# Transposing gathered rows by DMA, as two 16-bit halves, in a kernel of attention followed by routed experts

## The chip, the cores and the metric

The kernel runs on one core of a Trainium2 chip. The core has a matrix engine (TensorE, PE in the profile), three engines for elementwise work (VectorE or DVE, ScalarE or ACT, GpSimd or POOL), a queue engine (SyncE or SP) and 16 DMA engines that all queues share. Each engine runs its own instructions in order; engines wait for each other by semaphores. The metric is the device time of one execution in microseconds (us). Before the change it is 213.47 us, the median of 3 runs from 212.46 to 213.69.

## The reference

There are two stages. The first is an attention with polynomial sketches; its output is put into rows of 128 numbers, one row for each of 4352 tokens. The second sends each row through one of eight experts, which a hash of the token's id selects:

```python
expert_idx = token_ids * np.int64(2654435761) % np.int64(E)
for e in range(E):
    mask = expert_idx == e
    xe = x[mask]
    h = np.maximum(xe @ w1[e], 0.0)
    out[mask] = h @ w2[e]
```

Here `x` is 4352 x 128, `w1[e]` is 128 x 1024 and `w2[e]` is 1024 x 128, all 32-bit floats.

## The kernel before

The attention stage handles four batches one after the other. For each it makes sketch features, sums them into a small matrix (`kv`), multiplies queries by it (`x_ps`), divides by a denominator (`den`, lines 460 and 461), and stores the rows (`xs`, line 466, and the rest of a batch, `xs_tail`, line 480) to a table `x_rows` in memory. Beside it, VectorE and TensorE work out a list of tokens sorted by expert: `get` holds, for each of 36 tiles of 128 slots, the rows to fetch, and `put` the rows to write.

The expert stage works on 16 groups of 288 columns, two for each expert. The first eight groups (18 tiles, 0 to 17) hold only tokens whose rows are stored early, so they can start before the last batch is done; tiles 18 to 35 need the whole table.

- **Gather.** `gather` (line 549) is an indirect DMA that GpSimd issues: 128 rows of 128 numbers into a tile `xg`. The tiles come from a pool of six buffers (line 576).
- **Transpose.** `bring` (lines 582 to 592) takes three gathered tiles at a time. TensorE transposes each of them into a bank of PSUM, `xp` (line 589). `evict` (line 553) copies the bank to columns of `xT`: ScalarE takes the even calls and VectorE the odd ones. `xT` is kept in blocks of nine tiles (1152 columns, four groups), in two buffers (line 569); so there are four blocks, and block 2 can be written only when block 0 has been read.
- **First product.** For each of eight steps c of a group, `hp` (line 664) is a 128 x 128 piece of `w1` times the group's 288 columns. It goes to one of four PSUM banks. Its relu goes to `hT` by ScalarE for even c (line 555) and by VectorE for odd c (line 557); that frees the bank.
- **Second product.** Interleaved with it, `op` (line 672) sums the eight pieces of the previous group times `w2`.
- **Send.** `send` (lines 644 to 656) lets TensorE turn finished columns back into rows (`tp`, line 650), copies them to `os`, and GpSimd scatters each tile to the output (`out_dram`, line 637).

At step c = 3 of each group g, lines 682 and 683 bring in all tiles up to the end of group g + 1. Up to line 628 the instructions of all engines stand in the order of the program text; that covers the attention stage and the first six gathers. After that line a scheduler decides in which order each engine has its instructions, and the order is then fixed. The pool `moe` (line 632), from which `hT`, `os` and the change's new tiles come, takes the memory that the attention stage's loads have released.

Of the kernel before, what the change touches and what calls it, by code (L numbers as in the profile page):

```python
# [9 lines left out]
F32 = mybir.dt.float32  # L10
BF16 = mybir.dt.bfloat16
I32 = mybir.dt.int32
AF = mybir.ActivationFunctionType
OP = mybir.AluOpType
AX = mybir.AxisListType
# [2 lines left out]
def _words(ap):  # L18

    t = dataclasses.replace(ap.tensor, shape=list(ap.tensor.shape))  # L20
    return t.bitcast(I32)


@with_exitstack
def kernel(
# [12 lines left out]
    nc = tc.nc  # L38
    P = 128
    B, H, S, D = q.shape  # L40
    R = S1.shape[0]
    N, DM = out.shape
# [13 lines left out]
    GN = 288  # L56
    EB = B - 2
    EP = (EB * S + SM // 2) // C
    NE = EP * C
    HT = E * GN // P  # L60
    ST = 2 * HT
# [6 lines left out]
    rows_in = ctx.enter_context(tc.tile_pool(name="rows_in", bufs=6))  # L68
# [14 lines left out]

    s64 = const.tile([2 * R, D, 2], I32)
    for i, s in enumerate((S1, S2)):
        nc.sync.dma_start(s64[i * R:(i + 1) * R], _words(s).rearrange("r (d two) -> r d two", two=2))
    tok = const.tile([P, C, 2], I32)
    nc.scalar.dma_start(tok[:], _words(moe_token_ids).rearrange("(p c two) -> p c two", p=P, two=2))

    def load_tail(src, name, eng):  # L90
# [82 lines left out]

    def s_tile(name, dt=I32):
        return const.tile([2 * R, D], dt, name=name)
# [53 lines left out]
    in_tile = hots.tile([P, C, ST], BF16)  # L229
    put = const.tile([P, ST], I32)  # L230
    get = const.tile([P, ST], I32)

# [315 lines left out]
    def gather(dst, idx, rows=N):  # L548
        nc.gpsimd.indirect_dma_start(  # L549
            out=dst[:], out_offset=None, in_=x_dram[0:rows],  # L550
            in_offset=bass.IndirectOffsetOnAxis(ap=idx, axis=0), bounds_check=rows - 1, oob_is_err=False)

    def evict(n, dst, src, relu=False):
        if n % 2 == 0:
            nc.scalar.activation(dst, src, AF.Relu if relu else AF.Copy)  # L555
        elif relu:
            return nc.vector.tensor_scalar(dst, src, 0.0, None, op0=OP.max).ins  # L557
        else:
            nc.vector.tensor_copy(dst, src)


    BG, BT = 4, 4 * GN // P
    assert BG * GN == BT * P and ST % BT == 0
    xTs, oTs = {}, {}

    def columns(of, pool, name, lo, hi):
        b = lo // (BT * P)
        if b not in of:
            of[b] = pool.tile([P, BT * P], F32, tag=name, name=name, bufs=2)
        return of[b][:, lo - b * BT * P:hi - b * BT * P]  # L570
# [3 lines left out]
    def fetch(upto):  # L574
        for i in range(len(xgs), upto):
            xg = rows_in.tile([P, DM], F32, tag="xg", name="xg")
            gather(xg, get[:, i:i + 1], NE if i < HT else N)
            xgs.append(xg)

    done_in = done_out = 0  # L580

    def bring(upto):
        nonlocal done_in
        while done_in < upto:
            n = min(3, ST - done_in)
            fetch(done_in + n)
            xp = ps_x.tile([P, 4, P], F32, tag="x", name="xp")
            for i in range(n):
                nc.tensor.transpose(xp[:, i], xgs[done_in + i][:], ident[:])  # L589
            evict(done_in // 3, columns(xTs, rows_in, "xT", done_in * P, (done_in + n) * P),  # L590
                  xp[:, 0:n].rearrange("p a b -> p (a b)"))
            done_in += n


    b, e = EB, EB + 1
# [24 lines left out]
    for g in range(GQ):  # L620
        x_products(e, g, fTs[g], last_m)
    bring(3)
    x_tail_products(e, last_m)
    denominators(e, 0, GQ * HQ + H)
# [7 lines left out]
    moe = ctx.enter_context(tc.tile_pool(name="moe", bufs=3))  # L632
# [11 lines left out]
    def send(upto):  # L644
        nonlocal done_out
        while done_out + 1 <= upto:
            n = min(2, upto - done_out)
            tp = ps_x.tile([P, 4, P], F32, tag="x", name="tp")
            for i in range(n):
                nc.tensor.transpose(tp[:, i], columns(oTs, moe, "oT", (done_out + i) * P, (done_out + i + 1) * P), ident[:])  # L650
            os = moe.tile([P, 2, DM], F32, tag="os", name="os", bufs=3)
            evict(done_out // 2, os[:, 0:n], tp[:, 0:n])
            for i in range(n):
                sent = scatter(os[:, i], put[:, done_out + i:done_out + i + 1])
            done_out += n
        return sent
# [3 lines left out]
    def layer1(g, c):  # L660
        if c == 0:
            hTs[g] = moe.tile([P, FC, GN], F32, tag="hT", name="hT", bufs=2)
        hp = bank([P, GN], "hp")
        nc.tensor.matmul(hp[:], w1[:, g % E, c * P:(c + 1) * P], columns(xTs, rows_in, "xT", g * GN, (g + 1) * GN), start=True, stop=True)  # L664
        return evict(c, hTs[g][:, c], hp[:], relu=True)
# [3 lines left out]
    def layer2(g, c, lo=0, hi=GN):  # L669
        if c == 0:  # L670
            ops[g] = ps_o.tile([P, GN], F32, tag="o", name="op")
        nc.tensor.matmul(ops[g][:, 0:hi - lo], w2[:, g % E, c], hTs[g][:, c, lo:hi], start=(c == 0), stop=(c == FC - 1))  # L672
        if c == FC - 1:
            nc.scalar.copy(columns(oTs, moe, "oT", g * GN + lo, g * GN + hi), ops[g][:, 0:hi - lo])  # L674

    G = 2 * E
    for g in range(G):
        for c in range(FC):
            last = layer1(g, c)
            if g > 0:  # L680
                layer2(g - 1, c)
            if c == 3:
                bring(min(ST, -(-((g + 2) * GN) // P)))
            if c == 3 and g > 1:
                sent = send((g - 1) * GN // P)
                if g % 4 == 3:

                    with tc.issue_after(sent):
                        nc.gpsimd.drain()
        if g == G - 4:  # L690
            tables_after = last
# [38 lines left out]
    with tc.For_i(0, turns) as j:  # L730
# [25 lines left out]
        xg = rows_in.tile([P, DM], F32, tag="xg", name="xg")  # L756
# [6 lines left out]
        for i in range(FH):  # L763
            hp = bank([P, 512], "hp")
            nc.tensor.matmul(hp[:], xr[:], w1f[:, bass.ds(e + i * 512, 512)], start=True, stop=True)
            nc.scalar.activation(hs[:, i * 512:(i + 1) * 512], hp[:], AF.Relu)
        hr = moe.tile([P, FC, P], F32, tag="hT", name="hr", bufs=2)
# [41 lines left out]
```

## Time and profile before

| What | Value |
|---|---|
| Span of the profiled run | 213.5 us |
| TensorE busy | 200.3 us, 94% |
| VectorE, ScalarE busy | 101.3 us (47%), 69.1 us (32%) |
| GpSimd busy | 96.8 us, 45% |
| First gather issued | 62.50 us |
| First hp | 71.27 us |
| Last gather, last scatter issued | 172.15 us, 208.02 us |
| TensorE's end, about | 206.6 us |

A row of the groups view names the line, engine and operation, the tile written and the tile read, the count, then the busy time in us and the mean duration in ns, and last the engine's idle time just before these instructions and what ended it. In the timeline a row begins with its start and the time it covers, both in us. A 32-bit matrix product stands as two records, and records of TensorE overlap, so the distance between starts says more of its pace than the durations. The idle time of an engine which is not the bottleneck costs nothing.

### The profile page before, as it was taken

How to read it: one execution, taken by the hardware profiler on the slowest of the kernel's cores; microseconds unless marked ns; L12 is line 12 of the kernel's file. 1: busy time of each engine (PE TensorE's matmuls, PEld its weight loads, DVE VectorE, ACT ScalarE, POOL GpSimd, SP SyncE). 2: the span in 40 equal slices, each digit the busy share in tenths (PEclk: the TensorE clock that was granted, in tenths of full speed). 3: DMA queues.
4: the chain of work that ended last, by engine and by line, in shares of the span. 5: the costliest groups of instructions: out<-in, count | busy, mean ns of one | idle time of the engine just before them, and what ended most of it. 6: DMA issues, size and time to landing. Idle time of an engine off the chain costs nothing.

```text
span 213.5 us, 3351 instructions
## 1 busy us (share of the span) xinstructions
PE 200.3 (94%) x1178; PEld 164.6 (77%) x1179; DVE 101.3 (47%) x204; ACT 69.1 (32%) x195; POOL 96.8 (45%) x118
## 2 busy tenths in 40 slices
PE   7889999999898989999999999999999999999960
PEld 2779999899788667777777777777777787777850
DVE  4599999999998141223223123132232228232200
ACT  2231843636334223322331242333213233322210
POOL 8253105227028787035467733376741550530371
PEclk9999999999999999999999999999999999999997
DMA  3999899999111331000111100111210100100000
GB/s 112 298 291 328 286 347 339 297 351 344 62 51 49 108 129 49 12 25 25 40 35 39 55 31 15 37 38 40 61 39 0 46 24 14 36 12 12 23 27 24
DMA packets 22177, 22.16 MB, mean 104 GB/s; under 512 B 4186, under 2 KB 19291, under 8 KB 22160
## 3 DMA queue, kind: packets, MB, share of 16 engines
q1 hardware_dynamic: 18496, 17.05, 26.0%
q0 software_dynamic: 2432, 4.72, 7.2%
q10 hardware_dynamic: 1232, 0.17, 0.5%
q8 instruction: 10, 0.16, 0.3%
q14 instruction: 7, 0.06, 0.1%
HBM read 17.47 MB, written 4.59 MB: 103 GB/s over the span
## 4 chain that ended last, share of the span: by engine, by line
PE 48%; DVE 21%; issue 11%; DMA 11%; POOL 4%; ACT 1%; POOLq 1%; SPq 1%; DVEq 0%; ACTq 0%
PE hp L664 22%; PE op L672 19%; DMA out_dram<-os,put 8%; DVE f L354 4%; DVE fT L427 3%; DMA q<-in_q_dram 3%; POOL out_dram L637 3%; DVE kp L354 3%; DVE qT L404 2%; PE kv L379 2%; DVE row L288 2%; PE xp L589 1%; PE x_ps L436 1%; PE tp L650 1%; PE x_ps L447 1%
## 5 line engine op out<-in xcount | busy, mean ns | idle before, releaser
L664 PE MATMUL hp<-xT,w 128*128 128x288 f32 x256 | 82.5, 408 | 1.0 <-DVE hT L557 1.0
L672 PE MATMUL op<-hT,w 128*128 128x288 f32 (+2 forms) x272 | 82.1, 392 | 0.0
L557 DVE TENSOR_SCALAR hT<-hp 128x288 f32<-128x288 f32 x64 | 29.3, 457 | 84.0 <-PE hp L664 65.6
L672 PEld LDWEIGHTS op<-hT,w 128*128 128x128 f32 x272 | 49.8, 191 | 12.4
L549 POOL DMA_INDIRECT xg<-x_rows,get x36 | 37.5, 1040 | 44.2 <-PE xp L589 16.1
L664 PEld LDWEIGHTS hp<-xT,w 128*128 128x128 f32 x256 | 47.1, 190 | 13.4 <-DVE hT L557 1.5
L637 POOL DMA_INDIRECT out_dram<-os,put x36 | 35.9, 996 | 36.9 <-ACT os L555 18.9
L555 ACT ACTIVATE hT<-hp 128x288 f32<-128x288 f32 x64 | 26.1, 410 | 61.0 <-PE hp L664 47.6
L466 POOL TENSOR_TENSOR xs<-xe,den 128x512 f32<-128x512 f32 x6 | 7.7, 1297 | 20.3 <-DVE den L461 12.6
L436 PE MATMUL x_ps<-m,fT 128*128 128x132 f32 x128 | 15.8, 280 | 0.0
L379 PEld LDWEIGHTS kv<-va,kp 128*128 128x128 f32 x128 | 14.7, 192 | 0.9 <-issue 0.7
L379 PE MATMUL kv<-va,kp 128*128 128x66 f32 x128 | 14.8, 274 | 0.5 <-DVE kp L354 0.5
L436 PEld LDWEIGHTS x_ps<-m,fT 128*128 128x128 f32 x128 | 14.8, 190 | 0.3
L398 ACT COPY m<-kv 32x66 f32<-32x66 f32 x48 | 9.9, 205 | 11.4 <-PE kv L379 10.8
L674 ACT COPY oT<-op 128x288 f32<-128x288 f32 (+2 forms) x17 | 6.5, 384 | 19.0 <-PE op L672 12.8
L354 DVE TENSOR_TENSOR f<-ab 128x1024 f32<-128x1024 f32 (+1 forms) x9 | 11.6, 1289 | 0.1
L427 DVE STREAM_TRANSPOSE fT<-f 128x1024 f32<-128x1024 f32 (+1 forms) x9 | 11.2, 1244 | 0.7
L354 DVE TENSOR_TENSOR kp<-ab 128x1024 f32<-128x1024 f32 x8 | 9.3, 1242 | 0.0
L342 PE MATMUL ab_ps<-s_k,kT 128*128 128x64 f32 (+1 forms) x72 | 9.1, 275 | 0.0
L165 PE MATMUL idle<-warm 128*128 128x512 bf16 x21 | 7.8, 486 | 1.4 <-POOL warm L137 1.4
L342 PEld LDWEIGHTS ab_ps<-s_k,kT 128*128 128x128 f32 (+1 forms) x72 | 8.6, 191 | 0.5 <-issue 0.2
L413 PE MATMUL abq_ps<-s_k,qT 128*128 128x64 f32 (+1 forms) x72 | 8.5, 269 | 0.4 <-DVE qT L404 0.4
(138 smaller groups left out, 151.2 us busy)
## 6 DMA issues: line engine op xcount, KB each, us to landing
w<-in_moe_w_dram SPq DMA_DIRECT2D x16, 512.0 KB, 8.1
k<-in_k_dram SPq DMA_DIRECT2D x4, 512.0 KB, 4.6
v<-in_v_dram SPq DMA_DIRECT2D x4, 512.0 KB, 7.9
q<-in_q_dram SPq DMA_DIRECT2D x3, 512.0 KB, 7.7
x_rows<-xs SPq DMA_DIRECT2D x3, 512.0 KB
xg<-x_rows,get POOLq DMA_INDIRECT x36
out_dram<-os,put POOLq DMA_INDIRECT x36
q<-in_q_dram SPq DMA_DIRECT2D x2, 256.0 KB, 6.9
```

Of the source, the lines that this page charges most:

```text
L342: nc.tensor.matmul(ab_ps[:, g:g + w, h].rearrange("p t x r -> p t (x r)"), kT[:w * D, h], s_k[:w * D, 0:w].rearrange("p t x r -> p (t x r) ...
L354: eng.tensor_tensor(dst, ab[:, :, 0].unsqueeze(3).to_broadcast(shape), ab[:, :, 1].unsqueeze(2).to_broadcast(shape), op=OP.mult)
L379: nc.tensor.matmul(kv[:, pr], kp[rows, t, 2 * pr:2 * pr + 2].rearrange("p h i j -> p (h i j)"), va[rows, t, 2 * pr:2 * pr + 2].rearrange(" ...
L398: copy(m[f][t * D:(t + 1) * D, h::2, t], src)
L427: nc.vector.transpose(fT[r].rearrange("p k (q s) -> p k q s", q=Q), f[r].rearrange("p q h (k d) -> p (h k) q d", d=D))
L436: nc.tensor.matmul(p[:, h], fT[:, (h0 + h) * FB + fb], m[fb][:, h0 + h].rearrange("p t d -> p (t d)"), start=(fb == 0), stop=(fb == FB - 1 ...
L549: nc.gpsimd.indirect_dma_start(out=dst[:], out_offset=None, in_=x_dram[0:rows], in_offset=bass.IndirectOffsetOnAxis(ap=idx, axis=0), bound ...
L555: nc.scalar.activation(dst, src, AF.Relu if relu else AF.Copy)
L557: return nc.vector.tensor_scalar(dst, src, 0.0, None, op0=OP.max).ins
L637: st_ = nc.gpsimd.indirect_dma_start(out=out[:], out_offset=bass.IndirectOffsetOnAxis(ap=idx, axis=0), in_=src[:], in_offset=None, bounds_ ...
L664: nc.tensor.matmul(hp[:], w1[:, g % E, c * P:(c + 1) * P], columns(xTs, rows_in, "xT", g * GN, (g + 1) * GN), start=True, stop=True)
L672: nc.tensor.matmul(ops[g][:, 0:hi - lo], w2[:, g % E, c], hTs[g][:, c, lo:hi], start=(c == 0), stop=(c == FC - 1))
```

## The change

The tiles of the first block (0 to 8) are brought in as before. All later tiles go another way: three gathers fill one tile `xg3`; two copies split each 32-bit word into its two 16-bit halves, `xh`; one DMA transpose on SyncE's queue turns all six 128 x 128 pieces of 16-bit words into `xh_turned`; two more copies join the halves in `xT`. It is meant to take the transposes of 27 tiles from TensorE. So that the longer way has time, tiles are brought in one group earlier: at c = 3 of group g, up to the end of group g + 2. `xg3` has three buffers, `xh` and `xh_turned` two each.

```diff
+def _half(ap, x):
+    return ap.bitcast(U16).rearrange("p (n two) -> p n two", two=2)[:, :, x]
...
             n = min(3, ST - done_in)
+            if done_in >= BT:
+                xg = moe.tile([P, 3, DM], F32, tag="xg3", name="xg3", bufs=3)
+                for i in range(n):
+                    gather(xg[:, i], get[:, done_in + i:done_in + i + 1], NE if done_in + i < HT else N)
+                xh = moe.tile([P, 2, 3 * DM], U16, tag="xh", name="xh", bufs=2)
+                tt = moe.tile([P, 2, 3, P], U16, tag="xh_turned", name="xh_turned", bufs=2)
+                for x in range(2):
+                    evict(done_in // 3, xh[:, x, 0:n * DM], _half(xg[:].rearrange("p a b -> p (a b)"), x)[:, 0:n * DM])
+                assert n == 3
+                nc.sync.dma_start_transpose(tt[:].rearrange("p x a b -> p (x a) b"), xh[:].rearrange("p x b -> p (x b)"))
+                to = columns(xTs, rows_in, "xT", done_in * P, (done_in + n) * P)
+                for x in range(2):
+                    evict(done_in // 3, _half(to, x), tt[:, x].rearrange("p a b -> p (a b)"))
+                done_in += n
+                continue
             fetch(done_in + n)
...
             if c == 3:
-                bring(min(ST, -(-((g + 2) * GN) // P)))
+                bring(min(ST, -(-((g + 3) * GN) // P)))
```

In the changed program's own line numbers the gather is line 555, the relus are lines 561 and 563, the split and join copies 561 and 565, the DMA transpose 602, the TensorE transpose 611, hp 686 and op 694.

More of the change, by code (lines that the diff above doesn't have):

```diff
@@ L12 @@
 I32 = mybir.dt.int32
+U16 = mybir.dt.uint16
 AF = mybir.ActivationFunctionType
```

## The prediction

> **What bounds the kernel now.** I read the page first: its chain that ended last, and its groups of instructions. One core gives the time, 213.5 us in the profile and 213.47 us as the median.
>
> ```profile
> PE hp L664 22%; PE op L672 19%; DMA out_dram<-os,put 8%; DVE f L354 4%; DVE fT L427 3%; DMA q<-in_q_dram 3%; POOL out_dram L637 3%; DVE kp L354 3%; DVE qT L404 2%; PE kv L379 2%; DVE row L288 2%; PE xp L589 1%; PE x_ps L436 1%; PE tp L650 1%; PE x_ps L447 1%
> ...
> L664 PE MATMUL hp<-xT,w 128*128 128x288 f32 x256 | 82.5, 408 | 1.0 <-DVE hT L557 1.0
> L672 PE MATMUL op<-hT,w 128*128 128x288 f32 (+2 forms) x272 | 82.1, 392 | 0.0
> ...
> L549 POOL DMA_INDIRECT xg<-x_rows,get x36 | 37.5, 1040 | 44.2 <-PE xp L589 16.1
> ```
>
> The two expert matrix products (hp, op) head the chain, and the idle time before them is 1.0 us and 0.0 us. GpSimd issues 36 gathers, with 44.2 us idle before them. Next the stages, by the view of windows:
>
> ```profile
> core 0: us, PE busy (x) PEld busy (x) DVE busy (x) ACT busy (x) POOL busy (x), PEclk, DMA share, GB/s
> 71.00:78.00 7.00, 5.89 (x28) 3.96 (x27) 2.64 (x7) 1.80 (x5) 5.63 (x8) 1.00 0.17 49
> 95.00:112.00 17.00, 17.00 (x77) 13.49 (x76) 4.66 (x11) 4.78 (x12) 8.42 (x9) 1.00 0.10 28
> 112.00:200.00 88.00, 88.00 (x388) 68.76 (x387) 27.25 (x67) 24.93 (x63) 41.66 (x42) 1.00 0.10 32
> ```
>
> From 78 us on TensorE has no gap at full clock; VectorE and ScalarE are under a third busy, the DMA engines a tenth. So in the expert stage each TensorE instruction removed is time gained, and each wait that holds up TensorE is time lost. Only the entry (71 to 78 us) has gaps. The timeline gives the price of a transpose:
>
> ```profile
> 96.94 0.65 PE L672 MATMUL op<-hT,w 128*128 128x288 f32 x2
> 97.43 0.49 PE L589 MATMUL xp<-ident,xg 128*128 128x128 f32 x3
> 97.76 0.38 PE L650 MATMUL tp<-ident,oT 128*128 128x128 f32 x2
> 97.97 0.65 PE L664 MATMUL hp<-xT,w 128*128 128x288 f32 x2
> ```
>
> Durations overlap, so I use starts. Three gathered tiles take 97.76 - 97.43 = 0.33 us, 0.11 us each. One hp or op (two records) takes 0.485 us, so one step c of a group (an hp and an op) takes 0.97 us. The same view at the entry:
>
> ```profile
> 70.03 1.00 POOL L549 DMA_INDIRECT xg<-x_rows,get  x1 [0.30 <-issue]
> ...
> 71.33 1.00 POOL L549 DMA_INDIRECT xg<-x_rows,get  x1 [0.30 <-issue]
> 72.64 1.00 POOL L549 DMA_INDIRECT xg<-x_rows,get  x1 [0.30 <-issue]
> ...
> 73.31 0.78 PE L589 MATMUL xp<-ident,xg 128*128 128x128 f32 x3
> ...
> 73.94 1.00 POOL L549 DMA_INDIRECT xg<-x_rows,get  x1 [0.30 <-issue]
> ```
>
> Gathers leave every 1.30 us, and TensorE is already at their heels: tile 5 (issued 70.03) is transposed about 73.76. I call gathered tiles 0 to 35; groups of 288 columns g; block 0 is tiles 0 to 8, groups 0 to 3.
>
> **What the Trainium skill says.** "VectorE: DVE Perf Modes", The three transpose paths, gives 1309 ns for a 128x128 bf16 transpose by DMA and 390 ns by TensorE; in this trace TensorE's cost 0.11 us in a row, so only the ordering agrees, and no DMA transpose is in the trace. "DMA: Bandwidth & Descriptors", Latency and other measured facts, gives 261 GB/s for such transfers. The same page, DMA Transpose (X-bar), limits them to 2-byte elements, which is why each 32-bit word is split. The same page, Rules for kernel authors, has a DMA that reads what another wrote wait for its completion; here gathers of tiles 18 up wait for the last batch's rows to be stored, and the trace shows a 256 KB store landing in 2.0 us.
>
> **The change, part by part.**
> 1. Removed from TensorE: 27 transposes x 0.11 = 2.9 us, all on the gapless part: -2.9 us. Their evictions (nine of 128x384: ScalarE 0.49, VectorE 0.56) go too.
> 2. Added: four copies of 128x384 for each of nine triples (two split, two join). No row shows a strided 16-bit copy; I take 0.49 as ScalarE's row, bounds 0.42 and 0.6. That is 36 x 0.49 = 17.6 us over two engines with over 60% idle in this stage. Their duration alone is hidden.
> 3. Added: nine transfers of 196 KB on SyncE's queue. Lower bound 2 us (196 KB / 261 GB/s = 0.75 us of data; the 256 KB store's 2.0 us), upper bound 6 x 1.309 = 7.9 us, both estimates from the page and the store row. I take 4 us, nearer the store.
> 4. Moved, and this decides. ScalarE and VectorE run in order and also free the four PSUM banks of hp: a copy waiting for a gather holds the relu behind it, and TensorE stops about four steps later. GpSimd's queue is in order too. In the built program's order GpSimd issues tiles 0-5, then **tiles 9-15, then 6-8**, then the last batch's rows, then 16-35; every scatter follows. TensorE has tile 6's transpose ahead of hp(g=0, c=4), tile 7's ahead of c=5, tile 8's ahead of c=6, because block 0 is now brought in one group earlier.
>
> Entry: the gathers from 71.33 on are tiles 9, 10, ..., 15, 6, 7, 8. Tile 8 leaves at 71.33 + 9 x 1.30 = 83.06 instead of 73.94. For landing I take 3.3 us from the issue's start, range 2.9 to 3.7 (tile 5 above gives 3.7; the rows' tail, which waits for tile 8, starts 77.09, so at most 3.15 there). Tile 8 lands at 86.4; hp(0,6) 86.5, hp(1,1) 88.4. Before, hp(1,1) starts 78.45, and 0.33 more with tiles 6-8 transposed already, as they now are: +9.7 us. VectorE's copies for tiles 9-11 (landed 77.2) and ScalarE's for 12-14 (81.2) hold their relus too, but end earlier, so they hide in this wait.
>
> Groups 1 and 2: the last batch's rows (2.1 + 0.4 us on GpSimd) wait for tile 8 and end 86.8; stored and landed by about 89.5 (2.0 to 4 us). Tile 18 can leave then. Twelve gathers at 1.30 put tile 29 at 89.5 + 11 x 1.30 = 103.8, landed 107.1. VectorE has the copies for tiles 27-29 right after relu (2,1) and ahead of relu (2,3): copies to 108.1, relu to 108.6. hp(2,7) needs that bank, so it starts 108.6. Before it starts at 92.58, with the same nine tiles transposed: +16.0 us in all. Waits between (tile 17, 91.5; the third transfer, about 96; tile 23, about 99; tile 26, about 103) lie inside that sum. Later copies have their gathers landed (tile 35 at about 115) and wait for a transfer alone, with some 3 us of slack: nothing at 4 us.
>
> Scatters: the first leaves at about 113 instead of 90.5. By then four to six tiles are due, at 1.30 us each against 2.25 tiles per 8 us: caught up long before the end. TensorE's end to the span's end, 213.5 - 206.6 = 6.9 us, stays.
>
> Sum: 213.5 + 16.0 - 2.9 = **226.5 us**.
>
> **Rivals.**
> - All hidden, as intended: tiles 6-8 are needed only for columns 576 up, so the earlier order costs nothing: 213.5 - 2.9 = 210.6. For: DMA a tenth busy, helpers idle. Against: gathers leave 1.30 us apart and seven stand ahead of tile 6, on the one engine that issues them. Faster; 4%.
> - Only the entry's wait: copies of groups 1 and 2 fit in the slack of four banks: 213.5 + 9.7 - 2.9 = 220.3. For: VectorE is mostly idle. Against: tile 29's landing. 15%.
> - Slow transfers, 7.9 us: the transfer of tiles 21-23, from about 104, must release the buffer that 27-29 split into (+4), and in groups 4 and 8 the joining copy stands two or one relus behind the one that starts its transfer (+2.5 each): about 236. For: the only price per tile. Against: the store row. 14%; slower still, with transfers queueing behind each other, 5%.
> - The forecast: 60%. Another 2% for gains and losses that cancel.
>
> **How the numbers follow.** The forecast moves with landing (0.8 us over its range), store (2 us) and copies (1 us): 223 to 230. The low end reaches the entry-only case less its landing error, 219.5; the high end the 7.9 us transfers and a little, 238. Outside lie the hidden case, the very slow one, and parts of others. Faster by over 1% 4%, within 1% 2%, slower 94%.
>
> **What would show it.** Right: TensorE idle some 10 us between hp(0,3) and hp(0,7), ended by gathers; tile 8's gather near 83; then idle before hp in groups 1 and 2 laid to VectorE and ScalarE relus behind copies; hp(2,7) near 108; gapless after, at 0.97 us a step without L589 rows; transfers landing in 2 to 6 us. Wrong: gathers closer than 1.3 us, an entry gap under 7 us, or idle that recurs in groups 4 and 8 (slow transfers). Largest risk: a transfer's duration, which no row before shows.

## The result, and the profile after

The changed kernel takes 229.75 us (median of 4 runs, 227.43 to 230.6), the kernel before 213.12 us beside it (212.46 to 213.69). The ratio is 1.076, with a 95% interval of 1.068 to 1.085: slower, by some 16 us. The profiled run has a span of 228.9 us. Times of later kernels are compared with the kernel before as run on the same chip (213.8 to 214.4 us). Some runs come out slower at a lower clock; they are left out of every ratio, though not of the medians.

The page first, its slices and its groups:

```profile
PE   7979999999989049968799999999999999999980
...
PEclk9999999999999755999799999999999999999995
...
L686 PE MATMUL hp<-xT,w 128*128 128x288 f32 x256 | 86.2, 423 | 4.9 <-DVE hT L563 4.2
L694 PE MATMUL op<-hT,w 128*128 128x288 f32 (+2 forms) x272 | 83.6, 398 | 0.0
...
L555 POOL DMA_INDIRECT xg<-x_rows,get x36 | 37.1, 1030 | 22.9 <-DVE f L360 10.4
...
L611 PE MATMUL xp<-ident,xg 128*128 128x128 f32 x9 | 2.4, 337 | 9.8 <-DMA xg<-x_rows,get 9.7
```

TensorE has a hole in the 14th and 15th slices (74 to 86 us), and thinner slices from there to about 114 us; the clock falls to 0.5 in the 15th and 16th. The idle time is 9.8 us before the nine transposes that are left, and 4.9 us before hp, where it was 1.0. Next the stages, cut as before at 71, 95, 112 and 200 us, with the piece between 78 and 95 added:

```profile
core 0: us, PE busy (x) PEld busy (x) DVE busy (x) ACT busy (x) POOL busy (x), PEclk, DMA share, GB/s
71.00:78.00 7.00, 3.00 (x21) 2.25 (x19) 1.00 (x4) 0.68 (x2) 5.22 (x6) 0.96 0.19 49
78.00:95.00 17.00, 11.24 (x32) 7.56 (x33) 3.88 (x11) 4.77 (x11) 11.91 (x13) 0.62 0.40 103
95.00:112.00 17.00, 12.10 (x48) 8.62 (x47) 4.56 (x13) 4.45 (x12) 13.04 (x14) 0.99 0.34 73
112.00:200.00 88.00, 88.00 (x372) 68.70 (x371) 27.51 (x71) 27.62 (x69) 27.91 (x29) 0.98 0.11 31
```

All of TensorE's idle time in these stretches lies before 112 us. From 95 to 112 us TensorE works 12.1 of 17 us instead of all of them. Between 78 and 95 us the granted clock is 0.62, a second loss that busy time does not show. After 112 us TensorE is full again. In none of these stretches are the DMA engines half busy. Who holds it up is in the timelines. GpSimd first:

```profile
71.54 1.00 POOL L555 DMA_INDIRECT xg<-x_rows,get  x1 [0.30 <-issue]
...
83.42 0.99 POOL L555 DMA_INDIRECT xg<-x_rows,get  x1 [0.30 <-issue]
84.42 2.06 POOL L472 TENSOR_TENSOR xs<-xe,den 128x512 f32<-128x512 f32 x2
87.03 0.40 POOL L486 TENSOR_TENSOR xs_tail<-xe,den 64x128 f32<-64x128 f32 x1 [0.54 <-POOL xs L472]
...
92.13 1.00 POOL L555 DMA_INDIRECT xg<-x_rows,get  x1 [2.05 <-DMA x_rows<-xs_tail]
...
106.44 1.00 POOL L555 DMA_INDIRECT xg<-x_rows,get  x1 [0.30 <-issue]
...
115.53 1.02 POOL L659 DMA_INDIRECT out_dram<-os,put  x1 [0.30 <-issue]
```

These are, by count, tile 9's gather (71.54), tile 8's (83.42), the last batch's rows, tile 18's gather, which waits until the rows are stored, tile 29's (106.44), and the first scatter. TensorE beside it:

```profile
73.51 0.49 PE L611 MATMUL xp<-ident,xg 128*128 128x128 f32 x3
83.38 0.45 PE L611 MATMUL xp<-ident,xg 128*128 128x128 f32 x1 [9.38 <-DMA xg<-x_rows,get]
...
86.60 0.47 PE L611 MATMUL xp<-ident,xg 128*128 128x128 f32 x1 [0.37 <-DMA xg<-x_rows,get]
...
103.07 0.75 PE L686 MATMUL hp<-xT,w 128*128 128x288 f32 x2 [2.33 <-DVE hT L563]
...
107.18 0.75 PE L686 MATMUL hp<-xT,w 128*128 128x288 f32 x2 [0.71 <-ACT hT L561]
...
110.28 0.75 PE L686 MATMUL hp<-xT,w 128*128 128x288 f32 x2 [1.87 <-DVE hT L563]
...
112.14 1.17 PE L694 MATMUL op<-hT,w 128*128 128x288 f32 x2
```

First it waits 9.38 us for tile 6's rows, then three times for a relu: hp(2,3) at 103.07, hp(2,6) at 107.18, hp(2,7) at 110.28. A relu takes under half a microsecond, so the question is what the relu's engine was doing. VectorE:

```profile
102.00 0.66 DVE L565 COPY xh<-xg 128x384 uint16<-128x384 uint16 x2 [5.09 <-DMA xg<-x_rows,get]
102.58 0.81 DVE L563 TENSOR_SCALAR hT<-hp 128x288 f32<-128x288 f32 x2
...
109.23 0.63 DVE L565 COPY xh<-xg 128x384 uint16<-128x384 uint16 x2 [5.85 <-DMA xg<-x_rows,get]
109.78 0.81 DVE L563 TENSOR_SCALAR hT<-hp 128x288 f32<-128x288 f32 x2
```

It was idle, for 5.09 and 5.85 us: a split copy stood first in its queue and waited for a gather, with two relus behind it. TensorE's hp starts 0.49 and 0.50 us after those relus start. Between these two, hp(2,6) waited for ScalarE, which shows the same:

```profile
105.90 0.94 ACT L561 ACTIVATE xh<-xg 128x384 uint16<-128x384 uint16 x2 [6.54 <-DMA xg<-x_rows,get]
106.74 0.39 ACT L561 ACTIVATE hT<-hp 128x288 f32<-128x288 f32 x1
```

So it is not true here that the idle time of an engine which is not the bottleneck costs nothing: work that TensorE needed stood behind it.

The new transfers and the copies that join the halves:

```profile
L565 DVE COPY xT<-xh_turned x10: 375/380/390, 81.6 to 157.0; 128x384 uint16<-128x384 uint16 x10
L602 SPq DMA_TRANSPOSE xh_turned<-xh x9: 1210/1219/1328, 77.8 to 153.9; - x9
L561 ACT ACTIVATE xT<-xh_turned x8: 605/620/643, 88.4 to 153.3; 128x384 uint16<-128x384 uint16 x8
...
DMA to landing us min/median/max: 2.7/3.0/3.8
```

A transfer of 196 KB lands 3.0 us after its issue (2.7 to 3.8), and SyncE takes 1.2 us to issue it.

The description of the kernel before needs one correction. Ahead of line 628 the text order holds for the instructions written there, but the scheduler also puts later gathers and copies among them. In the changed kernel that is where the gathers of tiles 9 to 15 and the first split copies stand.

### The profile page after: what moved, and what is told of

Same layout as the page of the kernel before. It is cut to its first block, busy times and chain, and to the rows that moved or that the text cites. A ratio compares the mean times of both kernels' runs of the same rounds, so it can differ in the third digit from the quotient of the medians.

```text
span 228.9 us, 3338 instructions
## 1 busy us (share of the span) xinstructions
PE 202.5 (88%) x1151; PEld 164.6 (72%) x1152; DVE 103.4 (45%) x219; ACT 74.3 (32%) x207; POOL 96.1 (42%) x118
## 4 chain that ended last, share of the span: by engine, by line
issue 34%; POOL 15%; DMA 11%; POOLq 2%
POOL out_dram L659 9%; DMA out_dram<-os,put 7%; POOL xg L555 6%; DMA xg<-x_rows,get 2%; DMA x_rows<-xs_tail 2%; POOLq L711 2%; POOL xs L472 1%; POOLq L659 0%; POOL xs_tail L486 0%; POOLq L555 0%; POOLq L486 0%; POOLq L752 0%
## 5 line engine op out<-in xcount | busy, mean ns | idle before, releaser
L686 PE MATMUL hp<-xT,w 128*128 128x288 f32 x256 | 86.2, 423 | 4.9 <-DVE hT L563 4.2
L694 PE MATMUL op<-hT,w 128*128 128x288 f32 (+2 forms) x272 | 83.6, 398 | 0.0
L659 POOL DMA_INDIRECT out_dram<-os,put x36 | 35.4, 983 | 74.5 <-ACT os L561 44.2
L686 PEld LDWEIGHTS hp<-xT,w 128*128 128x128 f32 x256 | 49.2, 199 | 18.4 <-DVE hT L563 5.1
L694 PEld LDWEIGHTS op<-hT,w 128*128 128x128 f32 x272 | 50.7, 193 | 13.2
L565 DVE COPY xh<-xg 128x384 uint16<-128x384 uint16 x10 | 3.2, 363 | 22.3 <-DMA xg<-x_rows,get 13.3
L611 PE MATMUL xp<-ident,xg 128*128 128x128 f32 x9 | 2.4, 337 | 9.8 <-DMA xg<-x_rows,get 9.7
L611 PEld LDWEIGHTS xp<-ident,xg 128*128 128x128 f32 x9 | 1.3, 155 | 11.8 <-ACT hT L561 9.6
L561 ACT ACTIVATE xh<-xg 128x384 uint16<-128x384 uint16 x8 | 3.7, 511 | 17.9 <-DMA xg<-x_rows,get 17.9
```

The lines of the kernel that those rows point to most:

```text
L659: st_ = nc.gpsimd.indirect_dma_start(out=out[:], out_offset=bass.IndirectOffsetOnAxis(ap=idx, axis=0), in_=src[:], in_offset=None, bounds_ ...
```

## The experiments

The theory: two orders lose the time. On GpSimd's queue, early gathers of later tiles delay tiles 6 to 8, and with them the rows of the last batch. On VectorE's and ScalarE's queues, split and joining copies wait ahead of relus that TensorE needs. The rivals: the earlier bringing-in costs by itself; or the transfers do, by their duration or by their traffic.

**The earlier lead alone** (lead_alone in the expectations). The kernel before, with its own TensorE transposes and only this:

```diff
-                bring(min(ST, -(-((g + 2) * GN) // P)))
+                bring(min(ST, -(-((g + 3) * GN) // P)))
```

> The kernel before, with only the earlier bringing: at c = 3 of group g the tiles up to the end of group g + 2, all transposed by TensorE. The theory (gathers of later tiles stand ahead of tiles 6 to 8 because their own buffers free them, and copies waiting for gathers hold up relus) expects almost nothing: the gathers still wait for TensorE to free six buffers, so tiles 6 to 8 leave at about 71 to 74 us; tile 8 lands near 76.7, half a microsecond after hp(0,6) could start: about 213.6 us, 213 to 215. A rival, that bringing tiles early is itself the loss because TensorE then waits for them, expects 220 us or more.

Measured: 216.88 us against 214.37 us, ratio 1.015 (1.009 to 1.021). Of its profile, the longest wait of TensorE for a gather, of three that sum to 2.6 us:

```profile
76.72 0.33 PE L589 MATMUL xp<-ident,xg 128*128 128x128 f32 x1 [1.50 <-DMA xg<-x_rows,get]
```

In this kernel the six buffers of `xg` keep later gathers behind tiles 6 to 8, which leave at 70.50 to 73.11 us. From the first hp to the first op it takes 8.39 us (70.44 to 78.83) instead of 6.69 (71.27 to 77.96); 0.33 of that is three transposes that only come earlier, so the lead costs about 1.4 us there. It is more than the theory had. The profiled run took 215.38 us at a mean clock of 0.993; the other three took 216.83 to 217.66 us at 0.979 to 0.981. So the rest of the 1.5% goes with a lower clock, and no trace shows where that drop lies or whether the lead causes it. Even with it, the lead is about a fifth of the whole loss: a part, not the cause.

**The old lead in the changed kernel**, halves and transfers kept:

```diff
-                bring(min(ST, -(-((g + 3) * GN) // P)))
+                bring(min(ST, -(-((g + 2) * GN) // P)))
```

> The changed kernel with its tiles brought in up to the end of group g + 1 again, as before the change; the halves and the transfers stay. If the loss comes from the order on GpSimd's queue and from copies that wait for gathers ahead of relus, the earlier bring is not what costs: in the built program GpSimd still has tiles 9 to 15 ahead of 6 to 8, and every copy of groups 1 and 2 still stands behind the same gathers. Only TensorE's transposes of tiles 6 to 8 come a group later, so it can do four more products before it waits, and then waits as long for the rows: 228 to 230 us. If the earlier bring itself is the loss, which lead_alone makes unlikely, the time falls to 220 or less.

Measured: 227.35 us (226.24 to 228.07) against 213.79, ratio 1.062 (1.055 to 1.070). TensorE's waits in its trace:

```profile
78.95 1.33 PE L686 MATMUL hp<-xT,w 128*128 128x288 f32 x2 [4.04 <-DVE hT L563]
83.31 3.25 PE L686 MATMUL hp<-xT,w 128*128 128x288 f32 x6 [3.03 <-ACT hT L561]
...
101.60 0.87 PE L686 MATMUL hp<-xT,w 128*128 128x288 f32 x2 [2.59 <-DVE hT L563]
102.26 1.17 PE L694 MATMUL op<-hT,w 128*128 128x288 f32 x2
...
108.78 0.75 PE L686 MATMUL hp<-xT,w 128*128 128x288 f32 x2 [1.13 <-DVE hT L563]
```

The wait for tiles 6 to 8 is gone from the entry, and 7 us of waiting for relus behind split copies stand in its place. This is what a chain with two holders looks like: take one away and the other shows. hp(2,7) comes at 108.78, only 1.5 us sooner, because tile 18's gather could leave at 90.50 instead of 92.13. The expectation had TensorE wait for the rows as long as before; it waited for relus instead, which were held by split copies of tiles 9 to 14. The time is a little under the expected 228 us, and the ratio is 1.062 instead of 1.076, so that the lead is again about a fifth of the loss; the rival's 220 us falls.

**Gathers of block 0 first.** In the changed kernel each later gather is queued behind tile 8's; the copies stay where the scheduler puts them:

```diff
+            got.append(gather(xg, get[:, i:i + 1], NE if i < HT else N).ins)
...
+                  with tc.issue_after(got[BT - 1]):
                     gather(xg[:, i], get[:, done_in + i:done_in + i + 1], NE if done_in + i < HT else N)
```

> The changed kernel with one edit: gathers of tiles 9 and up are queued on GpSimd behind that of tile 8. The theory expects the entry's wait of about 10 us gone (tile 8 leaves near 74 us), but VectorE and ScalarE still have the split copies in among the relus as in the changed kernel, so the waits of groups 1 and 2 remain, gated by gathers 1.30 us apart that start at about 77.9: by hand hp(3,1) near 107.6 us against 94.5 before and 113.1 in the changed kernel. With 2.9 us fewer transposes and perhaps 1.5 us of lower TensorE clock: about 224 us, 221 to 226. A rival, that the order of the first gathers is the whole loss, expects 210 to 212; a rival, that transfers and copies cost by themselves, expects no change from about 229.

Measured: 225.36 us (224.25 to 225.47), ratio 1.052 (1.045 to 1.058). Line 688 is hp here, and line 613 the transpose:

```profile
76.54 0.33 PE L613 MATMUL xp<-ident,xg 128*128 128x128 f32 x1 [1.29 <-DMA xg<-x_rows,get]
...
83.96 0.75 PE L688 MATMUL hp<-xT,w 128*128 128x288 f32 x2 [0.78 <-DVE hT L563]
...
88.60 1.33 PE L688 MATMUL hp<-xT,w 128*128 128x288 f32 x2 [3.40 <-ACT hT L561]
...
104.20 0.86 PE L688 MATMUL hp<-xT,w 128*128 128x288 f32 x2 [3.32 <-ACT hT L561]
```

The entry is mended (waits of 0.24, 0.87 and 1.29 us instead of 9.38), and most of the loss stays, as waits for relus. hp(3,1) came at 108.91 us, expected near 107.6. The copies' order is thus a loss of its own.

**Copies late, gathers left.** The reverse: the three stages of a triple are written apart: the three gathers first (`take`), the two split copies and the transfer a group and a step later (`split`), the two joining copies almost a group after that (`join`). The copies are held in the order of the text. Tiles 6 to 8 are brought with the old lead, and GpSimd still has the gathers of tiles 9 to 15 ahead of theirs:

```diff
+    AT = (0, 1, 2, 4, 5, 6, 8, 9, 10)
...
+                if (g, c) == (at, 5):
+                    take(j)
+                if (g, c) == (at + 1, 6):
+                    split(j)
+                if (g, c) == (at + 2, 5):
+                    join(j)
```

> The changed kernel with the work in stages: split copies one group after their gathers and join copies another group later, each queued behind the relus that the program has ahead of it; gathers of tiles 9 to 15 stay ahead of tiles 6 to 8, and TensorE has tiles 6 to 8 at step 3 of group 1, as in the kernel before. The theory expects only the entry's wait: tile 8 lands near 86.6 us where TensorE could use it at 81.4, so 5.2 us, and about 1.9 us for the lower TensorE clock after a gap of over 5 us: 213.1 + 5.2 + 1.9 - 2.9 = 217.3 us, 215.5 to 219, no waits for VectorE or ScalarE later. A rival, that transfers and copies cost by themselves, expects 223 or more.

Measured: 218.77 us, ratio 1.018 (1.010 to 1.027). All of TensorE's waits between 70 and 118 us:

```profile
83.69 0.30 PE L595 MATMUL xp<-ident,xg 128*128 128x128 f32 x1 [3.49 <-DMA xg<-x_rows,get]
84.93 0.47 PE L595 MATMUL xp<-ident,xg 128*128 128x128 f32 x1 [0.93 <-DMA xg<-x_rows,get]
86.38 0.48 PE L595 MATMUL xp<-ident,xg 128*128 128x128 f32 x1 [0.98 <-DMA xg<-x_rows,get]
```

They sum to 5.4 us, where 5.2 were expected, and the clock is low after them (0.53 from 86.65 to 92 us). No relu is waited for; what is left is the gathers' order.

**Both orders put right** (staged_in_order). The last kernel, and the gathers queued one behind the other between the scatters (`queued` also holds the first nine gathers and every scatter):

```diff
+            with tc.issue_after(queued[-1]):
+                queued.append(gather(xg3s[j][:, i], get[:, lo + i:lo + i + 1], NE if lo + i < HT else N).ins)
```

> As the staged kernel, and the gathers of tiles 9 and up queued on GpSimd behind tile 8 and between the scatters: both waits of the theory are removed, and all of the change's transfers and copies stay. The theory expects TensorE gapless and 27 transposes fewer: 213.1 - 2.9 = 210.2 us, 209.5 to 211. A rival, that transfers and copies cost by themselves, expects 216 or more; a rival, that some slower GpSimd queue or landing now bounds the end, expects 213 to 215.

Measured: 210.24 us against 214.37, ratio 0.981 (0.976 to 0.987), faster than both kernels. That is some 4 us (2.8 to 5.2) where 2.9 were expected; the expected 210.2 was reckoned from 213.1 us, so that it was met so closely is in part luck. The profile is of a run of 212.17 us whose clock was low in the attention stage (0.74 from 40 to 50 us); from 50 us on it is 1.00. One wait of 0.31 us for a gather is left in the expert stage, and none for a transfer. The ratios side by side: neither order right 1.076, gathers alone 1.052, copies alone 1.018, both 0.981. The two gains sum to 0.082, together they bring 0.095. That each order hides a part of the other's loss is seen in the trace of the kernel with the old lead, not in this difference: the ratios' intervals are as wide as it is, and the last two kernels also bring tiles 6 to 8 with the old lead.

What the removed transposes are worth can be read off the groups' pace, at ScalarE's copy of each finished group. Before, and then this kernel:

```profile
126.93 0.40 ACT L674 COPY oT<-op 128x288 f32<-128x288 f32 x1 [1.04 <-PE hp L664]
135.24 0.40 ACT L674 COPY oT<-op 128x288 f32<-128x288 f32 x1 [1.04 <-PE hp L664]
```

```profile
126.96 0.40 ACT L680 COPY oT<-op 128x288 f32<-128x288 f32 x1 [1.04 <-PE op L678]
134.94 0.40 ACT L680 COPY oT<-op 128x288 f32<-128x288 f32 x1 [0.22 <-PE op L678]
```

A group takes 8.31 us with three transposes and 7.98 without: 0.33 us for each of nine triples, 3.0 us. From the first such copy to the last it is 120.2 us before (85.77 to 205.97) and 116.8 here (86.94 to 203.72), 3.4 less; the other 0.4 us I did not resolve.

**Each transfer twice** (transfers_twice), in the last kernel, and that kernel again beside it (staged_again):

```diff
-        nc.sync.dma_start_transpose(tts[j][:].rearrange("p x a b -> p (x a) b"), xhs[j][:].rearrange("p x b -> p (x b)"))
+        for _ in range(2):
+            nc.sync.dma_start_transpose(tts[j][:].rearrange("p x a b -> p (x a) b"), xhs[j][:].rearrange("p x b -> p (x b)"))
```

> As staged_in_order, with each of the nine transfers issued twice into the same tile, so that a joined half comes about 1.2 to 3 us later and the DMA engines move 1.8 MB more. If nobody waits for a transfer and their traffic costs nothing, the time stays within 0.4 us of staged_in_order. If transfers cost by themselves (contention with gathers, scatters or weights, or a wait of a joining copy), it is 2 us or more above.

> The same kernel as staged_in_order, on the chip of transfers_twice, for the comparison: 210.2 us (209.5 to 211). Its TensorE end lies 2.9 to 3.5 us ahead of the kernel before.

Measured: 210.78 us with double transfers (ratio 0.981, 0.974 to 0.989) and 211.06 us with single ones (0.983, 0.976 to 0.990). They can't be told apart: 1.8 MB more on the DMA engines cost nothing that shows. With runs that spread over 2 us, a cost of 0.4 us, the bound that was expected, could not be seen; one of 2 us or more would. In the trace of the doubled kernel TensorE waits for no transfer, and its last work begins at 202.3 us instead of 206.3. For the end that the second expectation names there is no comparable trace. The rival that transfers cost 2 us or more by themselves falls for this kernel.

## Why the prediction was right

The mechanism held: the gathers' order at the entry, then split copies ahead of relus until tile 29 has landed, then no loss. The time lies 3.3 us above the forecast, within its range (its sum comes to 226.6, not 226.5). By its steps, as they are numbered there, and read in the two profiles, whose spans differ by 15.4 us where the medians differ by 16.6:

1. *Removed transposes, -2.9 us.* Shown in the kernel without waits: 3.0 us by the groups' pace.
2. *Copies, 0.49 us, hidden as duration.* VectorE's split took 0.36 us and its joining copy 0.38, ScalarE's 0.51 and 0.62. The durations are hidden: with the copies late, TensorE waits for none of them.
3. *Transfers, 4 us (2 to 7.9).* 3.0 us. The price in the Trainium skill ("VectorE: DVE Perf Modes", The three transpose paths) can't be multiplied by the number of pieces: six times 1309 ns would be 7.9 us, an estimate. The prediction's "only the ordering agrees" had no DMA transpose to rest on; here it does agree: three tiles take 3.0 us by DMA and took 0.33 us on TensorE.
4. *Moved, +9.7 us at hp(1,1), +16.0 at hp(2,7).* Tile 8's gather left at 83.42, forecast 83.06, and TensorE's gap is 9.38 us, forecast some 10. hp(1,1) came at 90.71 instead of 88.4, and hp(2,7) at 110.28 instead of 108.6, +17.7 us against the kernel before:

```profile
92.58 0.65 PE L664 MATMUL hp<-xT,w 128*128 128x288 f32 x2
```

Tile 18's gather left 2.6 us late, at 92.13 instead of 89.5. About 1 us of that came back: tile 29's rows were split 2.8 us after their gather left, not 3.3, and copies and relu took 1.1 us, not 1.5. So the term that failed in size is the store, "stored and landed by about 89.5". The last batch's rows ended at 87.43, not 86.8, and their store held tile 18's gather for 4.7 us more, where 2 to 4 were allowed. The forecast had the price of a 256 KB store, 2.0 us; the last batch's store is one of 512 KB and a tail of 32 KB, and a 512 KB store of this trace lands after 3.8 us (median).

What no step had is the clock. TensorE stopped at 74.0 us, the clock fell about 3.4 us later (0.70 from 77 to 78 us, 0.50 after), and TensorE ran at half clock for 8 us after the 9.38 us gap. It did so again, for 3.6 us, after the three waits in group 2:

```profile
83.40:91.40 8.00, 7.62 (x18) 4.69 (x19) 0.92 (x2) 2.72 (x6) 5.50 (x6) 0.52 0.46 129
110.20:118.50 8.30, 8.21 (x28) 6.20 (x29) 2.19 (x6) 1.63 (x4) 6.34 (x7) 0.79 0.20 51
```

The first drop explains most of hp(1,1): four products from 86.87 us on took 3.84 us instead of 1.94. It was then absorbed, since hp(2,3) waited for VectorE anyway, and VectorE for a gather. The second stretched four products from 1.94 to 3.63 us, 1.7 us that stay. The Trainium skill has this ("TensorE: Matmul & The Clock Gate", Part 1: The HAM clock gate): an idle window of some 3.4 us halves the clock, and about as much busy time brings it back. The first fall agrees with it, but its 8 us are more than twice that time, and the second drop came after waits of at most 2.33 us, which the window does not explain. A step that predicts a long wait of TensorE has to add the clock.

The sum as it came: 213.5 + 17.7 at hp(2,7), then 112.42 us from there to TensorE's last start plus its 0.33, instead of 114.03, which is -1.6 (-3.3 without the clock, forecast -2.9), and a tail of 6.2 us instead of 6.9: 228.9 us.

The rivals. *All hidden* gave 210.6 us, and the kernel with both orders right takes 210.24: the idea was sound, the order was not. *Only the entry* falls, since mending the entry left 225.4 us. *Slow transfers* falls by the 3.0 us, and since its sign, idle time of TensorE in groups 4 and 8, is missing: TensorE is full from 112 us on.

## What to carry to other kernels

Before work is moved from a full engine to idle ones, look at where the new instructions stand in those engines' queues: an instruction that waits for a DMA holds all that is behind it, and an engine a third busy can still stop the full one. Fetching earlier was no gain here, where one queue issues every gather; queue what is needed first in front, and put the waiting steps of a chain apart, each late enough that its input has landed. When the loss has two holders in a row, mend both before judging the idea.

## What was not expected of the hardware

- The half clock came after a single gap of 2.59 us (the kernel with the old lead: 0.50 from 102.2 to 105.5 us), but not after one of 2.33 us (the changed kernel at 103.07: 1.00 until 107.2). After the next two waits of the changed kernel, 0.71 and 1.87 us, it came too. All of these are shorter than the window of some 3.4 us that the Trainium skill gives in the same place, so that window does not explain these drops, and no run here tests what does.
- A store of 32 KB, issued 0.9 us after one of 512 KB on the same queue, held a gather for 4.7 us in the changed kernel. With the old lead the same store, issued at 87.56 and 0.7 us after the larger one, let tile 18's gather leave at 90.50, so it held it for 2.9 us at most. What makes the difference is open.
- On ScalarE the strided copy of 128x384 16-bit words took 0.62 us when it wrote with a stride and 0.51 when it read with one; on VectorE the two differ by 0.02 us.
